# Attention with top-k masking and two feed-forward stages on one core: score fill, lead weights and the closing products of the first block are put in another order

## The chip, the cores and the metric

The program runs on one core of one Trainium2 chip. The metric is the device time of one execution in microseconds (us). Three runs of the kernel before gave 1180.0 us in the median, 1177.77 to 1182.78. A core has a matrix engine (PE, with its weight loads as PEld), a vector engine (DVE), a scalar engine (ACT), a general engine (POOL) and a queue engine (SP) from which the transfers are issued. Each engine takes its own instructions in order, and engines wait for each other by semaphores.

## The reference

Four batches with eight heads of 576 tokens and 64 dimensions go through attention that keeps, in each row of scores, the 32 largest; the result (2304 tokens by 512 features) goes through two feed-forward stages with 2048 hidden units each.

```python
scores = scale * np.matmul(q, k.transpose(0, 1, 3, 2))
kth = np.partition(scores, -top_k, axis=-1)[..., -top_k:-top_k + 1]
scores = np.where(scores >= kth, scores, -1000000000.0)
scores = scores - np.max(scores, axis=-1, keepdims=True)
attn = np.exp(scores)
attn = attn / (np.sum(attn, axis=-1, keepdims=True) + 1e-09)
x = np.matmul(attn, v)                 # then transposed to (2304, 512)
h = np.maximum(x @ w_in, 0.0)          # first stage
x = h * h @ w_out
h = x @ w_in                           # second stage, own weights
out = np.maximum(0.01 * h, h) @ w_out
```

## The kernel before, in words

**Tiles.** The tokens are cut into nine units (`UNITS`), each unit into four head pairs (`uh`), each head pair into tiles of 128 score rows by 576 keys. Two tiles make a pair, numbered `p`; there are 72 pairs. Products run in a split form: a high part and a rest, so that a value is carried in two matrices (`xh` and `xl`, two halves of `wi` and `wo`).

**One tile's way.** PE makes the scores into PSUM (`scores`, L310), ACT copies them to a score buffer `s0` to `s5` (L311). DVE searches the 32 largest in seven operations: MAX finds eight, MATCH_REPLACE strikes them out into `w`, four MAX and three MATCH_REPLACE in all (L951, L953). ACT drops what is below the 32nd (`drop`, L329) and takes the exponential (L333); PE transposes the result (`pt_main`, L369), ACT copies it to `PT` (L379), and PE multiplies it with the values (`av`, L455). `x_out` scales by the reciprocal sum (L486), and writes the features `xh` (ACT, L487) and `xl` (L493).

**Fill.** The scores of batches 2 and 3 (`EARLY`), and of the unit `KEPT`, are made ahead. PE makes them into the PSUM tag `sp`, ACT copies them to one of five buffers of the tag `stage`, and SP stores them to memory (`sd`, L314). They are spread evenly over the slots of `FILL`.

**Blocks.** The tokens make six blocks. The first has 512 tokens, and is complete after pair 15 (`first_done`). Its last pair is not masked and multiplied with the pair as a whole, but tile by tile in `close`: subtraction for the shift (L347, twice), drop, exponential, reciprocal (L351), transposes (L369, L355, L357). The value product of the last head pair is done in two halves: the first head with `hs` = (0,), the second with (1,). The copy that writes the last `xh` is noted as `closed`.

**Weights.** A stage of a block takes 16 steps, and each step needs a chunk `wi` and a chunk `wo`. Chunks arrive as 64-bit numbers (`w_raw`, 1 MB each, two buffers) and are made into the split form when first used: ACT reads the low words (L565) and the high words (L574), DVE joins them (`bits`, L581), ACT and POOL split (L585, L586). For steps 0 and 1 this is done ahead by `lead_passes` (L606, on ACT) and `lead_bits` (L613, on DVE). After that, `w_convert` of step i+2 runs beside the products of step i, and the raw chunk of step i+4 is asked for when step i is done. The low words of step 2 are held behind `closed`.

**What sets the order.** A table of slots (`at(slot, fn)`, 16 slots a pair) says when each function is called. Calls are handed to a scheduler, with priorities (`SOON`, `URGENT`, `SEAM`), which places the instructions of each engine one after the other. `behind(key)` (L86 ff.) ties an instruction to stand after a noted one. A change in the table therefore moves instructions on all engines, also far from the place that was edited.

## Time and profile before

| what | value |
|---|---|
| median of three runs | 1180.0 us |
| lowest and highest | 1177.77 and 1182.78 us |
| the profiled execution's own time | 1180.58 us |
| its span, first to last instruction | 1178.8 us |
| PE busy | 1118.3 us, 95% |
| DVE busy | 838.6 us, 71% |
| ACT busy | 818.0 us, 69% |
| POOL busy | 747.9 us, 63% |
| mean granted PE clock | 0.989 |

The rows further below are from one profiled execution, and starts are counted from its first instruction. Busy times are averages over stages: up to about 165 us there is attention and fill alone, then block 0 closes, then the feed-forward steps of one block run beside the attention of the next, and after about 900 us there are feed-forward steps alone. A row of the timeline merges equal neighbours (x2), and where an engine stood idle before it, the brackets say how long and what released it. A product with `PT` stands once in the order and has two rows in the trace (five are x10).

### The profile page before, as it was taken

How to read it: one execution, taken by the hardware profiler on the slowest of the kernel's cores; microseconds unless marked ns; L12 is line 12 of the kernel's file. 1: busy time of each engine (PE TensorE's matmuls, PEld its weight loads, DVE VectorE, ACT ScalarE, POOL GpSimd, SP SyncE). 2: the span in 40 equal slices, each digit the busy share in tenths (PEclk: the TensorE clock that was granted, in tenths of full speed). 3: DMA queues.
4: the chain of work that ended last, by engine and by line, in shares of the span. 5: the costliest groups of instructions: out<-in, count | busy, mean ns of one | idle time of the engine just before them, and what ended most of it. 6: DMA issues, size and time to landing. Idle time of an engine off the chain costs nothing.

```text
span 1178.8 us, 20036 instructions
## 1 busy us (share of the span) xinstructions
PE 1118.3 (95%) x6376; PEld 985.8 (84%) x6376; DVE 838.6 (71%) x1770; ACT 818.0 (69%) x1827; POOL 747.9 (63%) x958
## 2 busy tenths in 40 slices
PE   5898977998899999999999999999999999999998
PEld 4777765877688899989998998888788899998997
DVE  7999999666775659999999999989999100110011
ACT  6999998998999668877677677656866633333322
POOL 7968746998888767767897776768656543002100
PEclk9999989999999999999999999999999999999999
DMA  9868767999999688899988888667676499779974
GB/s 306 283 216 284 259 206 268 355 325 330 333 340 366 222 309 291 278 317 384 308 288 294 297 286 292 228 215 234 223 234 207 147 327 337 264 244 347 349 257 134
DMA packets 108201, 329.53 MB, mean 280 GB/s; under 512 B 17216, under 2 KB 25408, under 8 KB 104000
## 3 DMA queue, kind: packets, MB, share of 16 engines
q1 hardware_dynamic: 105472, 323.53, 80.0%
q10 hardware_dynamic: 2624, 4.72, 1.1%
q8 instruction: 52, 0.85, 0.3%
q14 instruction: 53, 0.43, 0.1%
HBM read 257.03 MB, written 71.17 MB: 278 GB/s over the span
## 4 chain that ended last, share of the span: by engine, by line
PE 78%; ACT 9%; DVE 4%; POOL 3%; DMA 2%; issue 2%; ACTq 0%; POOLq 0%; DVEq 0%
PE h L675 31%; PE acc L714 16%; PE acc L712 15%; PE att L466 5%; PE att L369 4%; PE att L455 2%; DVE m L951 2%; PE sp L310 2%; DVE w L953 2%; PE att L310 2%; DMA wraw<-in_w_dram 1%; ACT e L333 1%; ACT stage L311 1%; PE att L384 1%; ACT s L311 1%
## 5 line engine op out<-in xcount | busy, mean ns | idle before, releaser
L675 PE MATMUL h<-xh,wi 128*128 128x512 f32 (+2 forms) x1280 | 345.1, 343 | 6.3 <-ACT ga L685 2.3
L951 DVE MAX8 m<-w 128x8 f32<-128x576 f32 x432 | 311.4, 748 | 2.3
L675 PEld LDWEIGHTS h<-xh,wi 128*128 128x128 f32 x1280 | 225.3, 189 | 31.8 <-ACT ga L692 3.6
L695 POOL TENSOR_TENSOR gl<-ga,gh 128x512 fp32r<-128x512 f32 (+2 forms) x160 | 162.5, 1018 | 124.8 <-ACT gh L694 106.4
L953 DVE MATCH_REPLACE8 w<-m,w 128x576 f32<-128x576 f32 x288 | 213.1, 743 | 0.7
L675 PE MATMUL h<-xl,wi 128*128 128x512 f32 (+2 forms) x640 | 204.5, 340 | 0.0
L377 POOL TENSOR_TENSOR PTs<-whole,PTs 128x512 fp32r<-128x512 f32 x112 | 144.8, 1300 | 45.7 <-ACT whole L376 43.7
L712 PE MATMUL acc<-gh,wo 128*128 128x512 f32 (+2 forms) x768 | 155.6, 340 | 0.0
L714 PE MATMUL acc<-wo,gh 128*128 128x512 f32 x576 | 152.4, 397 | 0.0
L712 PEld LDWEIGHTS acc<-gh,wo 128*128 128x128 f32 x768 | 126.1, 189 | 11.3
L675 PEld LDWEIGHTS h<-xl,wi 128*128 128x128 f32 x640 | 120.2, 189 | 10.8
L329 ACT ACTIVATE e<-s,m 128x576 f32<-128x576 f32 x144 | 112.4, 782 | 21.0 <-DVE m L951 14.4
L695 DVE TENSOR_TENSOR gl<-ga,gh 128x384 fp32r<-128x384 f32 x32 | 17.9, 559 | 151.8 <-ACT gh L694 149.1
L692 ACT ACTIVATE ga<-h 128x512 f32<-128x512 f32 (+2 forms) x96 | 46.6, 492 | 112.0 <-PE h L675 109.7
L951 DVE MAX8 m<-s 128x8 f32<-128x576 f32 x144 | 104.4, 748 | 26.4 <-ACT s L311 24.3
L714 PEld LDWEIGHTS acc<-wo,gh 128*128 128x128 f32 x576 | 104.9, 188 | 20.1
L333 ACT ACTIVATE e<-e,nb 128x576 f32<-128x576 f32 x144 | 111.3, 778 | 3.0 <-POOL nb L323 2.8
L953 DVE MATCH_REPLACE8 w<-m,s 128x576 f32<-128x576 f32 x144 | 106.9, 744 | 0.4
L687 POOL TENSOR_TENSOR ga<-ga 128x512 f32<-128x512 f32 (+2 forms) x80 | 66.3, 831 | 42.7 <-ACT gh L686 40.8
L466 PE MATMUL att<-PTs,VT 128*128 128x256 f32 (+2 forms) x504 | 87.9, 299 | 4.1 <-DVE PTs L394 2.4
L369 PE MATMUL att<-ident,e 128*128 128x128 f32 x576 | 86.8, 275 | 4.8 <-ACT e L333 4.4
L364 POOL TENSOR_SCALAR e<-e,rc 128x576 f32<-128x576 f32 x112 | 82.9, 752 | 11.7 <-DVE rc L341 9.8
(109 smaller groups left out, 2069.7 us busy)
## 6 DMA issues: line engine op xcount, KB each, us to landing
wi<-wd SPq DMA_DIRECT2D x160, 512.0 KB, 5.3
wo<-wd SPq DMA_DIRECT2D x160, 512.0 KB, 5.2
wraw<-in_w_dram SPq DMA_DIRECT2D x32, 1024.0 KB, 7.8
sd<-stage SPq DMA_DIRECT2D x76, 288.0 KB, 3.2
s<-sd SPq DMA_DIRECT2D x76, 288.0 KB, 5.1
wd<-wi SPq DMA_DIRECT2D x32, 512.0 KB, 7.3
wd<-wo SPq DMA_DIRECT2D x32, 512.0 KB, 7.3
vd<-VT SPq DMA_DIRECT2D x16, 640.0 KB, 6.5
```

The source lines that it names most:

```text
L329: ACT.activation(t["e"], t["s"], AF.Prelu, bias=pr["m8"][:, i, 31:32], scale=-1.0, alpha=1.0 / FAR)
L333: ACT.activation(e, e, AF.Exp, bias=pr["nb"][:, i:i + 1], scale=-FAR, accum_out=pr["sum"][:, i:i + 1])
L364: POOL.tensor_scalar(e, e, pr["rc"][:, i:i + 1], 1.0, op0=OP.mult, op1=OP.mult)
L369: PE.transpose(ps[:, j * P:(j + 1) * P], t["e"][:, j * P:(j + 1) * P], ident)
L377: POOL.tensor_tensor(pts[:, 4:8, c:c + P], whole, pts.bitcast(F)[:, 0:4, c:c + P], op=OP.subtract)
L466: PE.matmul(ps, lhsT=l, rhs=r, start=i == 0, stop=i == len(mm) - 1)
L675: PE.matmul(two[r][:, 0:n], lhsT=ws[r][:, w, c * P:(c + 1) * P], rhs=x[c][y][:, 0:n], start=cnt == mine[0], stop=cnt == mine[-1])
L695: (DVE if j >= GLD else POOL).tensor_tensor(gl[:, 0:n], a[:, 0:n], gh.bitcast(F)[:, 0:n], op=OP.subtract)
L712: PE.matmul(acc[c][:, 0:n], lhsT=wo[:, w, cs], rhs=g[:, 0:n], start=first, stop=last)
L714: PE.matmul(acc[c], lhsT=g[:, cs], rhs=wo[:, w, :], start=first, stop=last)
L951: cur["dve"] = DVE.max(out=m8[:, x, 8 * r:8 * r + 8], in_=t["s"] if r == 0 else t["w"])
L953: cur["dve"] = DVE.match_replace(out=t["w"], in_to_replace=m8[:, x, 8 * r:8 * r + 8], in_values=t["s"] if r == 0 else t["w"], imm_value=NEG)
```

## The change

The fill of early scores ends at slot 205, where it ended at 222. The lead passes of steps 0 and 1 begin at slots 206 and 212 (before 224 and 230), with their loads 40 slots ahead of that as before. Their high words go to a buffer of the tag `stage` in SBUF, where they went to PSUM. The scores of pair 16 use the PSUM tag `sp`, those up to pair 15 the tag `sd`. The second head's half of the last value product of block 0 is cut into its two tiles (`av_tile`, `x_tile`): one tile is multiplied, scaled and written while the other is still on its way. Of pair 16, the first MAX of each tile stands behind the last shift as before; the further search stands behind the last `xl`, and its drops behind `closed`.

```diff
--- before.py
+++ after.py
@@ -47,7 +47,7 @@
 KEPT = 3
 
 EARLY = (2, 3)
-FILL = (2, 222)
+FILL = (2, 205)
 KPB = 2
 NST = 5
 SDB = 2
@@ -302,7 +302,9 @@
         mm = [(x[:, h, c:c + P], kt[:, h, ks]) for h, c in t["parts"] for x in d]
         if not direct(uh):
             ps = stage_psum.tile([P, 512], F, tag="sp", name="sp", bufs=SPB)
-        elif t["i"] // 2 <= first_done + 1 or kept(uh):
+        elif t["i"] // 2 == first_done + 1:
+            ps = stage_psum.tile([P, 512], F, tag="sp", name="sp", bufs=SPB)
+        elif t["i"] // 2 <= first_done or kept(uh):
             ps = stage_psum.tile([P, 512], F, tag="sd", name="sd", bufs=SDB)
         else:
             ps = bank()
@@ -326,7 +328,8 @@
     def drop(pr, i):
         t = pr["t"][i]
         t["e"] = ebufs[t["i"] % NE]
-        ACT.activation(t["e"], t["s"], AF.Prelu, bias=pr["m8"][:, i, 31:32], scale=-1.0, alpha=1.0 / FAR)
+        with behind("closed") if pr["p"] == first_done + 1 else ExitStack():
+            ACT.activation(t["e"], t["s"], AF.Prelu, bias=pr["m8"][:, i, 31:32], scale=-1.0, alpha=1.0 / FAR)
 
     def expo_sum(pr, i):
         e = pr["t"][i]["e"]
@@ -455,6 +458,14 @@
             PE.matmul(ps, lhsT=vt[0:np_, j, h * D:h * D + P], rhs=PT[0:np_, j, uh["c0"] + h * n:uh["c0"] + h * n + n],
                       start=m == 0, stop=m == len(order) - 1)
 
+    def av_tile(uh, t):
+        vt = VT[uh["b"], uh["hp"]]
+        uh["avt"] = bank()
+        for j in range(5):
+            np_ = P if j < NJ else LEFT
+            PE.matmul(uh["avt"][:, 0:P], lhsT=vt[0:np_, j, D:D + P], rhs=PT[0:np_, j, t["col"]:t["col"] + P],
+                      start=j == 0, stop=j == 4)
+
     def av_split(uh, h):
         n = uh["n"]
         c = slice(uh["c0"] + h * n, uh["c0"] + h * n + n)
@@ -470,6 +481,21 @@
         mine, other = slice(h * 64, h * 64 + 64), slice(64 - h * 64, 128 - h * 64)
         ACT.activation(uh["tmp"][mine, 0:n], ps[other], AF.Copy)
         DVE.tensor_tensor(uh["xf"][mine, 0:n], ps[mine], uh["tmp"][mine, 0:n], op=OP.add)
+
+    def x_tile(uh, t):
+        blk = blocks[cur["fill"]]
+        xh, xl = block_x(blk)[uh["hp"]]
+        r0 = (t["i"] - uh["ti"]) * P - uh["n"]
+        r, x = slice(D, P), early.tile([P, 256], F, tag="xn", name="xn", bufs=1)
+        d = slice(uh["u"]["g0"] - blk["g0"] + r0, uh["u"]["g0"] - blk["g0"] + r0 + P)
+        DVE.tensor_tensor(x[r, 0:P], uh["avt"][r, 0:P], uh["rb"][r, r0:r0 + P], op=OP.mult)
+        closed = ACT.activation(xh[r, d], x[r, 0:P], AF.Copy)
+        cur["xl"] = DVE.tensor_tensor(xl[r, d], x[r, 0:P], xh.bitcast(F)[r, d], op=OP.subtract)
+        if r0:
+            assert uh["u"]["g0"] + uh["n"] == blk["g0"] + blk["n"]
+            cur["closed"] = closed
+            ready.append(blk)
+            cur["fill"] += 1
 
     def x_out(uh, hs):
         g0, n, hp = uh["u"]["g0"], uh["n"], uh["hp"]
@@ -600,8 +626,7 @@
         for x, w in enumerate(w_alloc(i)):
             xs = slice(x * 512, x * 512 + 512)
             lo, hi, b = raw[:, xs, 0], raw[:, xs, 1], c[:, xs]
-            v = stage_psum.tile([P, 512], F, tag="sd" if len(led) == 2 and not led[i] else "sp", name="v",
-                                bufs=SDB if len(led) == 2 and not led[i] else SPB)
+            v = ahead.tile([P, S], F, tag="stage", name="v", bufs=NST)[:, 0:512]
             ACT.activation(b, lo, AF.Copy, scale=L_SCALE, bias=L_BIAS)
             ACT.activation(v, hi.bitcast(F), AF.Prelu, scale=H_SCALE, alpha=2.0 ** 32)
             led[i].append((b, v.bitcast(U), w))
@@ -881,9 +906,14 @@
         tight = uh["last"] // 2 == first_done
         apart = uh["n"] > P and (uh["n"] % P or tight) and uh["ti"] % 2 == 0
         for hs in ((0,), (1,)) if apart else ((0, 1),):
-            near = tight and hs[-1] == 1
+            near = tight and hs == (1,)
             z = 16 * (uh["lastA"] // 2 if hs == (0,) else uh["last"] // 2) + (15 if near else 23 if tight and apart else 30)
             nq = 2 * len(hs)
+            if near:
+                for i, t in enumerate(pairs[first_done]["t"]):
+                    at(z - 7 + 8 * i, urgent(av_tile), uh, t)
+                    at(z - 6 + 8 * i, urgent(x_tile), uh, t)
+                continue
             for i in range(nq):
                 at(z + i, urgent(av) if tight else av, uh, hs, i)
             at(z + nq, urgent(x_out) if tight else x_out, uh, hs)
@@ -900,7 +930,7 @@
         for _ in w_convert(i):
             pass
 
-    for i, z in enumerate((224, 230)):
+    for i, z in enumerate((206, 212)):
         at(z - 40, w_raw, i)
         at(z, lead_passes, i)
         at(16 * first_done + 13, lead_bits, i)
@@ -947,7 +977,7 @@
                 x, r, top = i // 7, i % 7 // 2, i % 7 % 2 == 0
             t = pr["t"][x % 2]
             if i < 14 and top:
-                with behind("shift") if p == first_done + 1 and r == 0 else ExitStack():
+                with behind("xl" if r else "shift") if p == first_done + 1 else ExitStack():
                     cur["dve"] = DVE.max(out=m8[:, x, 8 * r:8 * r + 8], in_=t["s"] if r == 0 else t["w"])
             elif i < 14:
                 cur["dve"] = DVE.match_replace(out=t["w"], in_to_replace=m8[:, x, 8 * r:8 * r + 8],
```

The first place is DVE, in the search of pair 13 (score buffers s2 and s3), during the attention ahead of the close. Before, from the first strike-out of s3 on:

```order
L951 MAX m8_2013<-w_2017 128x8
L951 MAX m8_2156<-w_2159 128x8
L953 MATCH_REPLACE w_2160<-m8_2156,s3_104 128x576
L953 MATCH_REPLACE w_2159<-m8_2156,w_2159 128x576
L951 MAX m8_2156<-w_2160 128x8
L951 MAX m8_2156<-w_2159 128x8
L953 MATCH_REPLACE w_2160<-m8_2156,w_2160 128x576
L953 MATCH_REPLACE w_2159<-m8_2156,w_2159 128x576
L341 RECIPROCAL rc_2015<-sum_2014 128x2
L486 TENSOR_TENSOR xn_2187<-att_2146,rb_1964 128x256
L951 MAX m8_2156<-w_2160 128x8
```

The same pair now:

```order
L983 MATCH_REPLACE w_2222<-m8_2219,w_2222 128x576
L981 MAX m8_2076<-w_2080 128x8
L981 MAX m8_2219<-w_2222 128x8
L983 MATCH_REPLACE w_2223<-m8_2219,s3_104 128x576
L983 MATCH_REPLACE w_2222<-m8_2219,w_2222 128x576
L981 MAX m8_2219<-w_2223 128x8
L981 MAX m8_2219<-w_2222 128x8
L983 MATCH_REPLACE w_2223<-m8_2219,w_2223 128x576
L981 MAX m8_2219<-w_2223 128x8
L983 MATCH_REPLACE w_2223<-m8_2219,w_2223 128x576
L981 MAX m8_2219<-w_2223 128x8
```

Before, operations on the two tiles of the pair, or on those of a neighbouring pair, take turns. Now tile `w_2223` has five operations in a row, each of which reads what the one ahead of it has written.

The second place is PE, from the transposes of block 0's last pair (e2 and e3 are its two tiles, `VN` the values, `rc` the reciprocal sums) to shortly ahead of the first feature product. Before:

```order
L369 MATMUL att_2448<-ident_66,e2_109 128x128
L455 MATMUL att_2460<-PT_115,VN_1110 128x256 x5
L369 MATMUL att_2448<-ident_66,e2_109 128x128 x3
L355 MATMUL sp_2454<-ident_66,e2_109 64x128
L369 MATMUL att_2481<-ident_66,e3_110 128x128 x4
L355 MATMUL sp_2487<-ident_66,e3_110 64x128
L357 MATMUL sp_2454<-ident_66,rc_2400 128x128
L455 MATMUL att_2504<-PT_115,VN_1110 128x256 x4
L310 MATMUL att_2531<-KT_1731,q00_77 128x288
L310 MATMUL att_2531<-KT_1731,q10_78 128x288
L455 MATMUL att_2504<-PT_115,VN_1110 128x256
L357 MATMUL sp_2487<-ident_66,rc_2400 128x128
```

Now (L458 is the product of the first head, L466 that of one tile, L372, L358 and L360 are the transposes):

```order
L372 MATMUL att_2448<-ident_66,e2_109 128x128 x4
L358 MATMUL sp_2454<-ident_66,e2_109 64x128
L408 MATMUL att_2434<-ident_66,rc_2324 128x128 x2
L458 MATMUL att_2460<-PT_115,VN_1144 128x256 x5
L466 MATMUL att_2467<-PT_115,VN_1144 128x128 x5
L360 MATMUL sp_2454<-ident_66,rc_2400 128x128
L358 MATMUL sp_2497<-ident_66,e3_110 64x128
L372 MATMUL att_2491<-ident_66,e3_110 128x128 x4
L360 MATMUL sp_2497<-ident_66,rc_2400 128x128
L466 MATMUL att_2520<-PT_115,VN_1144 128x128 x5
L312 MATMUL att_2541<-KT_1784,q00_77 128x288
L312 MATMUL att_2541<-KT_1784,q10_78 128x288
```

The first head's product stood within the transposes of tile e2, and a product of 256 columns closed the row; now the tile products stand one behind the copy of e2, one behind that of e3.

The third place is ACT, where `ga` of step 2 (L685, now L710) stands among the high words (L574, now L600). The chunk `wraw_2672` was that of step 5, `wraw_2625` that of step 4. Before:

```order
L574 ACTIVATE att_2709<-wraw_2625 128x512
L585 ACTIVATE wi_2680<-wc_2682 128x512
L329 ACTIVATE e3_110<-s5_106,m8_2777 128x576
L574 ACTIVATE att_2746<-wraw_2672 128x512
L574 ACTIVATE att_2770<-wraw_2672 128x512
L685 ACTIVATE ga_2703<-h_2676 128x512
L129 ACTIVATE VT_3114<-vraw_3115 128x5x64 x2
L686 ACTIVATE gh_2701<-ga_2703 128x512
```

Now `wraw_2635` is the chunk of step 4 and `wraw_2682` that of step 5:

```order
L710 ACTIVATE ga_2713<-h_2686 128x512
L600 ACTIVATE att_2702<-wraw_2635 128x512
L600 ACTIVATE att_2719<-wraw_2635 128x512
L591 ACTIVATE wc_2692<-wraw_2635 128x1024
L711 ACTIVATE gh_2711<-ga_2713 128x512
L336 ACTIVATE e0_107,sum_2515<-e0_107,nb_2760 128x576
L336 ACTIVATE e1_108,sum_2515<-e1_108,nb_2760 128x576
L600 ACTIVATE att_2756<-wraw_2682 128x512
```

The two reads of the chunk of step 5 stood ahead of `ga` and `gh` of step 2; now the first of them is seven rows behind that `ga`, and the second follows it.

## Rows read from the trace of the kernel before

**Rows 1.** The page: the span.

```profile
span 1178.8 us, 20036 instructions
```

**Rows 2.** Busy time by stretch: stretch, length, PE, PEld, DVE, ACT, POOL, PE clock, DMA share, GB/s.

```profile
10.00:165.00 155.00, 135.45 (x786) 111.42 (x785) 154.07 (x334) 141.92 (x393) 120.12 (x179) 0.99 0.78 258
165.00:210.00 45.00, 34.02 (x137) 25.81 (x135) 40.91 (x86) 38.05 (x86) 29.97 (x34) 0.85 0.78 271
210.00:330.00 120.00, 110.15 (x516) 89.87 (x515) 83.48 (x156) 108.97 (x207) 108.60 (x110) 0.97 0.94 336
330.00:900.00 570.00, 564.53 (x3316) 504.51 (x3315) 517.24 (x1111) 421.05 (x913) 422.58 (x531) 1.00 0.82 282
```

**Rows 3.** Waits of DVE, 9 to 170 us: total us, times, longest us.

```profile
DVE m L951 <- ACT s L311: 1.8, 3, 1.3
```

**Rows 4.** Timeline of DVE around the last search: start, duration, engine, line, operation, operands, count.

```profile
157.76 0.74 DVE L951 MAX8 m<-s 128x8 f32<-128x576 f32 x1
158.42 0.07 DVE L953 MATCH_VALUE_LOAD w<-m,s 128x8 f32 x1
...
159.21 0.74 DVE L953 MATCH_REPLACE8 w<-m,w 128x576 f32<-128x576 f32 x1
159.87 1.41 DVE L951 MAX8 m<-w 128x8 f32<-128x576 f32 x2
...
168.98 0.16 DVE L347 TENSOR_TENSOR nb<-m 128x1 f32<-128x1 f32 x1
...
172.57 0.76 DVE L951 MAX8 m<-w 128x8 f32<-128x576 f32 x1
173.37 0.09 DVE L953 MATCH_VALUE_LOAD w<-m,w 128x8 f32 x1
173.44 0.74 DVE L953 MATCH_REPLACE8 w<-m,w 128x576 f32<-128x576 f32 x1
174.22 0.76 DVE L951 MAX8 m<-w 128x8 f32<-128x576 f32 x1
```

**Rows 5.** ACT by line and shape, 60 to 160 us: count, total busy us, mean ns, idle before.

```profile
L311 ACT ACTIVATE stage<-sp 128x288 f32<-128x288 f32 x100 | 35.5, 434 | 2.2 <-PE sp L310 1.9
```

**Rows 6.** Timeline of ACT at the close of block 0.

```profile
172.97 0.81 ACT L333 ACTIVATE e<-e,nb 128x576 f32<-128x576 f32 x1
...
177.39 0.60 ACT L379 ACTIVATE PT<-att 128x512 f32<-128x512 f32 x1 [2.74 <-PE att L369]
...
182.88 0.41 ACT L487 ACTIVATE xh<-xn 64x256 fp32r<-64x256 f32 x1
```

**Rows 7.** Timeline of PE at the close; in brackets its idle time and what ended it.

```profile
156.65 2.52 PE L455 MATMUL att<-PT,VN 128*128 128x256 f32 x10
...
164.64 1.04 PE L369 MATMUL att<-ident,e 128*128 128x128 f32 x8
...
173.14 3.74 PE L455 MATMUL att<-PT,VN 128*128 128x256 f32 x10
...
182.27 2.08 PE L675 MATMUL h<-xh,wi 128*128 128x512 f32 x8
```

**Rows 8.** Busy time by stretch: five us in which the PE clock fell.

```profile
170.00:175.00 5.00, 3.78 (x10) 2.73 (x11) 4.48 (x10) 4.66 (x13) 4.35 (x5) 0.50 0.93 326
```

**Rows 9.** Timeline of PE, its three long waits after the first feature products.

```profile
191.18 0.53 PE L310 MATMUL att<-KT,q 128*128 128x288 f32 x2 [2.39 <-DVE wc L581]
...
200.45 1.20 PE L712 MATMUL acc<-gl,wo 128*128 128x512 f32 x4 [2.26 <-POOL gl L695]
...
205.70 0.50 PE L675 MATMUL h<-xh,wi 128*128 128x512 f32 x1 [1.92 <-ACT ga L685]
```

**Rows 10.** Timeline of ACT, the wait for the raw weights.

```profile
203.95 1.18 ACT L574 ACTIVATE att<-wraw 128x512 f32<-128x512 f32 x2 [2.61 <-DMA wraw<-in_w_dram]
```

**Rows 11.** Timeline of the SP queue, raw weights of steps 4 and 5.

```profile
189.36 0.45 SPq L543 DMA_DIRECT2D wraw<-in_w_dram  x1
...
195.16 0.35 SPq L543 DMA_DIRECT2D wraw<-in_w_dram  x1
```

## The prediction

> **What bounds the kernel now.** I read the busy times by stretch first, then the timelines of DVE, PE and ACT where one engine hands over to another, and at each place the wait that ends last. The span [rows 1] is 1178.8 of the 1180.58 us of the profiled execution, with 1.8 us around it, which I leave as they are. The sum below is made against 1180.58, which is 0.6 us above the median of 1180.0.
>
> Three regimes follow each other [rows 2]. From 10 to 165 us DVE is busy 154.07 of 155 us: the search sets the time. PE has 19.6 us to spare there, but ACT only 13.1. From 165 to 210 us no engine is full. Block 0 closes, PE is idle 11.0 of 45 us and runs at a mean granted clock of 0.85. From 210 us on PE is the engine to look at: 110.15 of 120 us, then 564.53 of 570. What PE gets earlier at 210 us should therefore reach the end, unless a later stage gives it back. DVE is busy 517.24 of those 570 us too, but it has 36.5 us free between 210 and 330 us, so work pushed there finds room.
>
> So the change can earn in the 45 us of the close, and can lose in the search ahead of it.
>
> **Part 1: the search ahead of the close.** Fill copies move forward. In ACT's order, the score copies of pairs 10 to 15 now have 6 to 10 more fill copies ahead of them than before, at 0.36 us each (35.5 us for 100) [rows 5]: 2.2 to 3.6 us of ACT work. The work is the same in sum. Before, DVE waited for a score copy three times, 1.8 us in all and 1.3 at most [rows 3], so ACT was just in time, and this is a cost where ACT falls behind DVE.
>
> But DVE falls behind as well. What shows it is how its operations follow each other [rows 4]. Where the next operation works on another tile, MAX is followed after 0.66 us (157.76 to 158.42), MATCH_REPLACE after 0.66 (159.21 to 159.87). Where the next one reads what this one wrote, it is 0.80 (172.57 to 173.37) and 0.78 (173.44 to 174.22). Such a link costs 0.12 to 0.14 us. Before the second shift, DVE's order had 2 of them; now it has 21, as the first of the order pieces shows. The operations are the same in number, and there is no idle time to take it up: 19 x 0.13 = 2.5 us, later by that. Bounds: 0, if the next tile would have been waited for anyway, and 5 us, if the copies make DVE wait as well (two more waits of 1.3 [rows 3]). I take +2.5, since the two delays run side by side.
>
> The Trainium skill, "VectorE: DVE Perf Modes", section "The DRAIN you can't avoid", says that after every vector operation the pipe is flushed before the next begins, and that chaining does not change this. By that a link costs nothing, and this part is 0. The trace does not agree: 0.66 against 0.80 and 0.78.
>
> **Part 2: the close.** Before, the second shift is done at 168.98 [rows 4], and the last xh starts at 182.88 [rows 6]: 13.9 us. What lay in it: the second exponential starts only at 172.97, since ACT had four high words of the lead passes (now earlier) in its queue; the value product of the first head took 3.74 us [rows 7] at a granted clock of 0.50, its lower level of 1.2 GHz [rows 8], where 2.52 us was its time at the full clock; and the product of the second head, with all 256 columns, waited for both tiles.
>
> Now, counted from the second shift: the first head's product needs the last copy of pair 14, which stands in ACT's order behind the first exponential; of its 0.60 [rows 6] some 0.4 is still to run. First head, ten passes, 3.1 us (between 2.52 and 3.74): 3.5. Product of the first tile, half the columns: 1.6, to 5.1. ACT has meanwhile run the second drop and exponential (0.8 each), ready by 3. Transposes of the second tile and of its reciprocal, seven at 0.13 (1.04 for eight): 6.0. Copy 0.6: 6.6. Product of the second tile 1.6: 8.2. Scaling on DVE, one score copy queued ahead of it on ACT, then xh, some 0.4 each [rows 6]: 9.4. With hand-overs that I can't price from a row, 10.5. That saves 3.4. Bounds: 0, if PE stays at the half clock throughout and ACT's copies come late, and 5.4, if PE runs at the full clock (8.5).
>
> The feature products need the last xh only after sixteen of them; they started at 182.27 [rows 7], so they are held by PE's own queue, and go as the tile products go.
>
> **Part 3: steps 2 to 5 of the first stage.** After that, PE waits three times for long [rows 9]: 2.39 us for a bank that DVE's joining of the words of step 2 frees, 2.26 for POOL's rest of the hidden values, 1.92 for ACT's ga. Together 6.57. The third is a transfer. ACT stood 2.61 us at the high words of step 5 [rows 10], whose load was issued at 195.16 [rows 11], with ga of step 2 queued behind it. In ACT's order now, ga and gh of step 2 stand ahead of that read, so this wait leaves PE's path. The first is covered as well: on PE the products of wo of step 0 now stand ahead of those of step 2. The second stays: POOL still has wi and wo of step 2 to split beside the hidden values. 2.39 + 1.92 = 4.3 us off. Bounds: 0, if POOL or the transfer takes the place, and 6.6.
>
> The wait that is added: pair 16's search stands behind the last xl, and eight of its operations stand ahead of the joining of step 2 on DVE, 5.4 us at 0.66 to 0.73. ACT's wi, POOL's split and PE's products of step 2 wait for them. PE has the eight products with wo of step 0 meanwhile, about 2 us, so I count nothing; without that cover it is up to 3 us, which is in the upper bound of part 3 (nothing saved). Pair 16's own drops come later, and nobody waits for them before DVE's free time [rows 2].
>
> **Edits at nothing.** The high words hold four of the five stage buffers until DVE has read them, so the last fill copy waits for a store: hidden by the wait for the second shift, else one wait like the longest of rows 3, 1.3 us. The other PSUM tag for pair 16 takes no instruction away.
>
> **Sum.** +2.5 - 3.4 - 4.3 = -5.2. 1180.58 - 5.2 = 1175.4 us, 4.6 us (0.39%) below the median.
>
> **The rivals.** About 0.5%, 5.9 us, is what a measurement of this kernel can tell from no change: below 1174.1 is faster, above 1185.9 slower.
>
> All three waits go, and PE gets its clock back. The stretch 165 to 210 lacks 15% of 45 us of clock [rows 2], 6.8 us; a third of it is 2.2. +2.5 - 3.4 - 6.6 - 2.2 = -9.7: 1170.9. For it: worked through queue by queue, step 3 comes earlier by more than my sum. Against it: POOL's queue is no shorter.
>
> The gain is given back by 330 us. In that stretch ACT is busy 108.97 and POOL 108.60 of 120 us, and the transfers 0.94 [rows 2]. If these set the pace of the steps rather than PE, and the new order of the whole program lines them up worse by 5 us (half as much again as PE's 9.85 us of idle time there), it is 1180. For it: the order changes on every engine well past the close. Against: an earlier start of the same steps moves transfers forward too, into 165 to 210, where they were at 0.78.
>
> Slower: the search waits for score copies. Place: the first MAX of each tile of pairs 10 to 15, 12 of them. Price: 0.9 us each, two to three fill copies [rows 5], 10.8 in all, as ACT has little free time [rows 2]. 10.8 + 2.5 - 7.7 = +5.6: 1186.2. It decides from about 0.4 us a tile on, where the gains are used up. Against it: the copies of the last pair have the same total work ahead of them as before, so ACT can't lose 11 us on the whole unless it also stands idle more.
>
> Links cost nothing, as when each operation is followed after the same time whatever it reads: part 1 is 0, 1172.9. The rows speak against it. This is the skill's rule of part 1.
>
> **How the numbers follow.** The forecast has 0.38 (its own range 1172 to 1179; 0.08 of it lies below 1174.1). All waits gone 0.27, given back 0.21, slower 0.09, links free 0.05. Faster: 0.27 + 0.08 + 0.05 = 0.40. Slower 0.09, and 0.01 from the given-back case: 0.10. The same: 0.50. Range: lower end 1167, below the second case by some of its bounds (all of parts 2 and 3 at their best, 5.4 and 6.6, without part 1, is 1168.6, and the clock beside it), upper end 1183, which leaves the search's case out: about 2 in 10 outside.
>
> **What would show it.** The second shift at about 171.5 us where it was at 168.98, DVE still without idle time and its MAX rows at 0.8 where they follow their own strike-out; the last xh about 10.5 us behind the shift; no ACT wait for wraw ahead of ga of step 2, and the first feature product of step 3, at 205.70 before [rows 9], at about 200.5. From there the gap between both timelines should stay near 5 us up to the end. It is wrong if the second shift is on time (links free) or past 175 (copies late), if PE's waits in rows 9 are replaced by others of their size, or if the gap at 200 us and the gap at the end differ by more than 3 us.

## The result, and the profile after

The changed kernel takes 1195.3 us (median of 6 runs, 1191.94 to 1197.53) against 1180.63 for the one before (6 runs beside them): ratio 1.0114, interval 1.0087 to 1.0141. It is slower by 14.7 us where 5.2 us of gain were forecast. Its profiled execution took 1192.64 us.

The busy time by stretch, with the columns of [rows 2]:

```profile
10.00:165.00 155.00, 133.13 (x760) 108.49 (x760) 147.23 (x315) 137.90 (x383) 114.19 (x171) 0.98 0.77 257
165.00:210.00 45.00, 36.12 (x170) 28.76 (x168) 40.07 (x84) 36.18 (x85) 31.50 (x34) 0.89 0.66 233
210.00:330.00 120.00, 111.10 (x509) 89.51 (x508) 88.02 (x168) 111.46 (x212) 111.30 (x114) 0.96 0.96 340
330.00:900.00 570.00, 558.22 (x3264) 497.87 (x3264) 517.02 (x1106) 417.86 (x909) 418.63 (x527) 0.99 0.82 280
```

Two places stand out. In the search DVE, full before, is idle for 7.8 of 155 us and has done 19 instructions fewer. And from 330 us on PE has lost 6.3 us of busy time and some clock. The close between them got better, as far as PE goes: 36.12 us busy at a mean granted clock of 0.89, where it was 34.02 at 0.85.

**The search.** These are DVE's waits from 9 to 180 us (total, times, longest), 9.0 us in all:

```profile
DVE m L981 <- ACT s L313: 4.5, 3, 2.2
DVE rc L344 <- POOL sum L343: 3.3, 3, 2.6
DVE rc L344 <- ACT sum L341: 0.7, 1, 0.7
DVE m L981 <- POOL nb L325: 0.5, 1, 0.5
```

Before, they were 2.0 us: the 1.8 of [rows 3] and one more line of the same view:

```profile
DVE rc L341 <- POOL sum L340: 0.2, 1, 0.2
```

The timeline of DVE, as in [rows 4], at the second shift and the close:

```profile
177.75 0.76 DVE L981 MAX8 m<-w 128x8 f32<-128x576 f32 x1
178.54 0.16 DVE L350 TENSOR_TENSOR nb<-m 128x1 f32<-128x1 f32 x1
...
182.00 2.48 DVE L638 SCALAR_TENSOR_TENSOR wc<-v,wc 128x512 uint32<-128x512 uint32 x2
...
188.74 0.29 DVE L491 TENSOR_TENSOR xn<-att,rb 64x128 f32<-64x128 f32 x1 [3.20 <-POOL xl L519]
...
190.47 0.29 DVE L493 TENSOR_TENSOR xl<-xn,xh 64x128 fp32r<-64x128 f32 x1 [0.37 <-ACT xh L492]
```

The second shift comes at 178.54 and not at 168.98: 9.56 us late, of which 2.5 were forecast.

**The close and the first steps.** The timeline of PE, as in [rows 7, 9]:

```profile
179.64 3.25 PE L458 MATMUL att<-PT,VN 128*128 128x256 f32 x10
182.82 1.57 PE L466 MATMUL att<-PT,VN 128*128 128x128 f32 x10
...
185.88 1.57 PE L466 MATMUL att<-PT,VN 128*128 128x128 f32 x10 [0.25 <-ACT PT L382]
...
187.75 2.00 PE L700 MATMUL h<-xh,wi 128*128 128x512 f32 x8
...
197.33 0.53 PE L312 MATMUL att<-KT,q 128*128 128x288 f32 x2 [2.87 <-ACT s L313]
...
207.47 0.39 PE L700 MATMUL h<-xh,wi 128*128 128x512 f32 x1
```

The first feature product is 5.5 us later than before (187.75, was 182.27), the first of step 3 only 1.8 us (207.47, was 205.70). So by 207 us the feed-forward products had made good most of the 9.56 us. The search of the next block had not: the strike-out that DVE began at 210.55 us before is 9.4 us late.

**Far behind it.** Here the rows show something that the prediction did not look at. First two stretches of the kernel before, then the same two of the changed one:

```profile
540.00:570.00 30.00, 30.00 (x192) 28.90 (x192) 29.66 (x66) 22.19 (x49) 25.01 (x36) 1.00 0.98 359
...
640.00:670.00 30.00, 30.00 (x171) 27.25 (x170) 29.79 (x65) 21.32 (x47) 21.85 (x28) 1.00 0.90 302
```

```profile
540.00:570.00 30.00, 25.78 (x161) 23.48 (x160) 28.80 (x64) 21.14 (x49) 21.00 (x30) 1.00 0.90 329
...
640.00:670.00 30.00, 26.38 (x138) 23.73 (x137) 27.68 (x61) 20.02 (x46) 20.30 (x27) 0.89 0.73 245
```

Before, PE was full at its upper clock in both. Now it is idle 4.2 and 3.6 us, and the clock of the second is 0.89; on 26.38 us of busy time that is another 2.9 us by my estimate. The clock fell after PE had stood idle for 2.15 us; from 645 to 650 us it is 0.53, near the lower of its two levels (1.2 GHz):

```profile
646.70 1.65 PE L700 MATMUL h<-xh,wi 128*128 128x384 f32 x4 [2.15 <-DVE xl L752]
```

```profile
645.00:650.00 5.00, 3.30 (x10) 3.30 (x11) 4.94 (x11) 1.81 (x5) 1.46 (x3) 0.53 0.75 258
```

What it waits for in the first, from PE's timeline, and the SP queue at that time:

```profile
549.03 0.96 PE L700 MATMUL h<-xh,wi 128*128 128x384 f32 x4 [1.40 <-DMA wi<-wd]
...
557.10 0.38 PE L477 MATMUL att<-PTs,VT 128*128 128x256 f32 x1 [1.20 <-ACT PTs L377]
558.43 0.97 PE L700 MATMUL h<-xh,wi 128*128 128x384 f32 x4 [0.95 <-ACT xh L513]
```

```profile
548.27 0.32 SPq L320 DMA_DIRECT2D s<-sd  x1
555.71 0.32 SPq L656 DMA_DIRECT2D wo<-wd  x1
```

At 549 a new block of tokens begins (its products are 384 columns wide). Part of its first products need features that the attention is only just finishing (xh of L513). SP issues nothing for 7.4 us; its next load, of `wo`, waits 7.3 of them for PE (L387, a transpose). In the order of before, the same products began at 547.83, behind the last of these features (xh at 545.51).

To follow this through the runs I took the same event in each trace: the second shift, then the first `gl` of the first stage (199.12 us before), and the `gl` that were at 326.53, 537.10, 732.35 and 1170.00. They follow the feed-forward steps; the column "search" follows the attention by DVE's strike-out that was at 536.27. The table has the difference to before in us, and the ratio of the times. A trace is one execution; executions of one kernel differ by up to 10.0 us, so offsets below 4 us say little at the end, and the ratios decide there.

| run | shift | 199 | 327 | search | 537 | 732 | 1170 | ratio (interval) |
|---|---|---|---|---|---|---|---|---|
| changed kernel | +9.6 | +2.0 | +3.4 | +7.8 | +1.1 | +13.2 | +12.0 | 1.0114 (1.0087 to 1.0141) |
| e1 fill205 | +10.0 | +3.8 | +7.1 | +14.2 | +12.8 | +19.8 | +18.8 | 1.0135 (1.0117 to 1.0152) |
| e2 close_only | +2.2 | -6.1 | -0.1 | +4.1 | +4.2 | +4.1 | +5.3 | 1.0040 (1.0025 to 1.0054) |
| e3 dup_early | +10.8 | +13.4 | +9.4 | +10.7 | +10.7 | +10.4 | +8.8 | 1.0069 (1.0055 to 1.0084) |
| e4 close_xn | +2.0 | -5.2 | -1.0 | -0.2 | -0.2 | -0.1 | -0.6 | 1.0009 (0.9992 to 1.0025) |
| e5 fewer_stores | +0.4 | +0.4 | -4.9 | -4.1 | -4.0 | -4.1 | -4.8 | 0.9989 (0.9973 to 1.0006) |
| e6 close_fewer | +0.2 | -7.7 | -3.5 | -2.1 | -2.1 | -2.1 | -1.7 | 1.0011 (0.9995 to 1.0026) |
| e7 reorder | +1.7 | +2.2 | +0.4 | +4.9 | -1.7 | +9.5 | +8.3 | 1.0088 (1.0064 to 1.0111) |
| e8 sum_on_act | +11.3 | +4.3 | +16.4 | +20.2 | +20.2 | +20.2 | +20.3 | 1.0171 (1.0150 to 1.0192) |
| e9 links | +10.7 | +4.9 | +8.2 | +14.5 | +3.5 | +15.0 | +14.7 | 1.0105 (1.0081 to 1.0130) |
| e10 late_order | +3.0 | +3.4 | -0.8 | +8.1 | -2.0 | +13.4 | +11.6 | 1.0067 (1.0047 to 1.0088) |
| e11 no_hold | +0.4 | -6.0 | -2.9 | -1.2 | -1.3 | -1.2 | -1.2 | 0.9993 (0.9978 to 1.0009) |
| e12 fill206 | +8.4 | +1.5 | +4.9 | +4.4 | +4.4 | +4.3 | +4.0 | 1.0031 (1.0013 to 1.0049) |
| e13 fill202 | +11.2 | +4.3 | +7.1 | +7.4 | +7.4 | +7.4 | +8.6 | 1.0066 (1.0047 to 1.0086) |

The changed kernel's columns around 537 are the first surprise: its feed-forward was nearly level there, and its search was 7.8 us late. Behind that point the feed-forward had to wait for it.

The traces also show from where on a run has the instruction order of before again. In e2 to e6, e8 and e11 to e13 that is so on every engine from 490 us on at the latest. In these nine both columns agree within 0.1 us, and the offset changes by -1.8 to +1.2 us from 537 to 1170. The changed kernel, e1, e7, e9 and e10 have another order up to about 950 us or longer. In these five the search is 1.4 to 11 us further behind than the feed-forward at 537, and the offset grows by 6.0 to 13.7 us up to 1170.

### The profile page after: what moved, and what is told of

Read it like the earlier page. It is cut to its first block, busy times and chain, and to the rows that moved or that the text cites. A ratio compares the mean times of both kernels' runs of the same rounds, so it can differ in the third digit from the quotient of the medians.

```text
span 1190.9 us, 20042 instructions
## 1 busy us (share of the span) xinstructions
PE 1125.3 (94%) x6386; PEld 989.4 (83%) x6386; DVE 841.9 (71%) x1772; ACT 817.5 (69%) x1828; POOL 747.3 (63%) x958
## 4 chain that ended last, share of the span: by engine, by line
PE 63%; ACT 11%; DVE 8%; DMA 7%; POOL 3%; issue 3%; ACTq 0%; POOLq 0%; SPq 0%; DVEq 0%
PE h L700 26%; PE acc L739 16%; PE acc L737 9%; DVE m L981 4%; PE att L477 4%; DVE w L983 3%; PE att L372 3%; DMA wraw<-in_w_dram 3%; ACT e L336 2%; PE att L458 2%; ACT stage L313 1%; ACT e L332 1%; DMA wi<-wd 1%; PE sp L312 1%; ACT s L313 1%
## 5 line engine op out<-in xcount | busy, mean ns | idle before, releaser
L700 PE MATMUL h<-xh,wi 128*128 128x512 f32 (+2 forms) x1280 | 346.2, 345 | 10.6 <-ACT ga L710 3.2
L700 PEld LDWEIGHTS h<-xl,wi 128*128 128x128 f32 x640 | 120.5, 190 | 10.5
L739 PEld LDWEIGHTS acc<-wo,gh 128*128 128x128 f32 x576 | 105.2, 188 | 20.3 <-ACT gh L719 0.3
L372 PE MATMUL att<-ident,e 128*128 128x128 f32 x576 | 89.8, 278 | 10.5 <-ACT e L336 9.7
```

The lines of the kernel that those rows point to most:

```text
L372: PE.transpose(ps[:, j * P:(j + 1) * P], t["e"][:, j * P:(j + 1) * P], ident)
L700: PE.matmul(two[r][:, 0:n], lhsT=ws[r][:, w, c * P:(c + 1) * P], rhs=x[c][y][:, 0:n], start=cnt == mine[0], stop=cnt == mine[-1])
L739: PE.matmul(acc[c], lhsT=g[:, cs], rhs=wo[:, w, :], start=first, stop=last)
```

## The experiments

**Which edit, and is it the search?** The theory was that the search's delay is carried to the end by DVE (A), the rivals that PE carries the close's gain (P), or that the new order behind the close does the harm (B).

```diff
-FILL = (2, 222)
+FILL = (2, 205)
```

> The kernel before with one number changed: the fill copies are spread up to slot 205 and not 222; the close, the lead passes and the holds are those of before. Theory A (the search carries it: what DVE is late by at the second shift reaches the end, because DVE is full again from about 450 us on): second shift near 178 us instead of 168.98, the close takes its 13.9 us as before, end 1190 us or a little more, ratio 1.008 to 1.010. Theory B (the loss of the change comes from the new order after the close, not from the search): second shift late all the same, but the end within 3 us of 1180.6. Theory C (the search is late because of the lead passes and the pair behind the close, not because of the fill): second shift before 172 us and the end at 1180.

This one number on the kernel before makes the search 10.0 us late and the whole 1.35% slower. So the fill alone is enough for the search's delay, without the lead passes or the holds (C falls). But the offset of 12.8 at 537 us grew to 19.8 at 732: more than A has.

```diff
-FILL = (2, 205)
+FILL = (2, 222)
```

> The changed kernel with the fill put back to slot 222: the close by tiles, the early lead passes and the holds stay. Theory A (search carries): second shift back at 169 to 170 us, the last xh 2 to 4 us earlier than before, and the end still at 1179 to 1181 us, since the blocks after the first wait for the attention and not for the close. Theory P (PE carries from 210 us on, as the prediction had it): the gain of the close and of the first steps reaches the end: 1173 to 1176 us. Theory B (the order after the close does it): between 1185 and 1195.

All the other edits without the fill: the features lead by 6.1 us at 199, as the prediction's parts 2 and 3 had it, and the lead is gone at 327. P falls: 1.0040, not a gain. Behind 537 us the offset stays within 1.2 us.

```diff
                     cur["dve"] = DVE.max(out=m8[:, x, 8 * r:8 * r + 8], in_=t["s"] if r == 0 else t["w"])
+                if 10 <= p < 14 and 0 < r < 3:
+                    with behind("dve"):
+                        DVE.max(out=spare, in_=t["w"])
```

> The kernel before with sixteen more MAX instructions in the search of pairs 10 to 13, whose results go to a spare tile that nobody reads: 16 x 0.66 = 10.6 us of DVE work ahead of the close, and the order of all engines after the close is that of before. Theory A and theory P: second shift at 177 to 180 us, and the whole of the delay at the end: 1189 to 1192 us, ratio 1.007 to 1.010. Theory B (a late close is made up again in DVE's 36 us of free time between 210 and 330 us): 1180 to 1183.

Time lost in the search does reach the end, for the most part: 10.8 us at the shift, 10.7 at 537, 8.8 at 1170, ratio 1.0069. DVE's idle time between 210 and 330 us makes up little of it. By this A holds, and alone it would explain some three fifths of the loss. One reservation: the order was expected to be that of before, and on every engine it differs from it up to about 485 us.

```diff
-        r, x = slice(D, P), early.tile([P, 256], F, tag="xn", name="xn", bufs=1)
+        r, x = slice(D, P), uh["xn"][:, r0:r0 + P]
...
             x = early.tile([P, 256], F, tag="xn", name="xn", bufs=1)
+            uh["xn"] = x
```

> As the close-only kernel, and the two products of the second head write their scaled values into the buffer that the first head's half already has, so the second scaling does not wait for POOL to have read it (3.20 us of DVE in the changed kernel). Last xh 2 to 3 us earlier than in the close-only kernel. Theory A: the end does not follow it, 1179 to 1181 us, within 0.1% of the close-only kernel. Theory P: 2 to 3 us less than the close-only kernel, 1170 to 1174.

This run missed its aim. In e2, POOL was done with the buffer in time and DVE did not wait for it, so there was nothing to take away (both runs have the fill of before): the first feature product comes 10.6 us after the shift, where it came 10.8. The 4 us between the ends of e2 and e4 arose at 340 us, with another order of DVE and ACT in between, and say nothing of the buffer.

**Where the lead of the close goes.** Theory T: the transfers, at 0.94 of their time from 210 to 330 us [rows 2], set the pace. e5 leaves out six stores on the kernel before, e6 on e4; the later blocks then load another step's weights, so part of the result is other (as in e7).

```diff
+    LEFT_OUT = [(0, f) for f in (9, 10, 11, 12, 13, 14)]
+    for layer, f in LEFT_OUT:
+        wdram[layer, f] = wdram[layer, 2]
...
+        if steps[i][1:] in LEFT_OUT:
+            return
```

> The kernel before, leaving out the stores of the split weights of steps 9 to 14 of the first layer (6 MB written between about 250 and 310 us; the later blocks load step 2's weights in their place, the same bytes, so part of the result is other). The order on the compute engines is that of before, instruction for instruction. Theory T (from 210 to 330 us the transfers set the pace of the steps): the first block's first layer ends 5 to 9 us earlier at 308 us, and this stays to the end: 1172 to 1176 us. Rival E (PE, ACT and POOL set the pace there): within 1 us of before at 308 us and at the end.

> The same six stores left out of the close-only kernel with the shared buffer; its order on the compute engines stays too. That kernel was 5.4 us ahead of before at 199 us, 1.2 us at 327 us and 0.8 us at the end. Theory T (the lead is lost to transfers that were full anyway): the lead over the kernel before with the same stores left out stays 3 us or more at 327 us and at the end. Rival E (the lead is lost on PE's order, where feature products stand between search and transposes that are late): no lead over it at the end, within 1 us.

T falls. The transfers' share from 210 to 330 us went from 0.94 to 0.82, and the time did not move (0.9989, e6 1.0011). The single trace of e5, the fastest of its twelve runs, shows 4 us; the twelve do not. e6 led by 7.7 us at 199 and by 2.1 at 537, no more than e5.

**The order of the late part.** Leaving out another set of stores moved the order of all engines far behind the close, and that was the run that turned the case.

```diff
+    LEFT_OUT = [(0, f) for f in (7, 9, 11, 13)]
+    for layer, f in LEFT_OUT:
+        wdram[layer, f] = wdram[layer, f - 1]
```

> The kernel before, leaving out the stores of steps 7, 9, 11 and 13 of the first layer (4 MB). With this set the late part of the order (from about 700 us on, and much of 450 to 700) comes out as in the kernel of before with the fill up to slot 205, while the search ahead of the close is that of before. Theory A alone (only what DVE is late by at 450 us counts): at 504 us not later than before, and the same offset at the end, 1172 to 1181 us. Theory B as a second part (the new order costs some 5 us of its own between 550 and 850 us): the offset grows by 4 to 7 us between 537 and 833 us, end 1180 to 1186 us.

Less work, a search within 1.7 us at the shift, feed-forward 1.7 us ahead at 537 (its search 4.9 behind), and then 11 us lost up to 732: 1.0088. B holds as a second cause, and in this trace its price is about twice what I had written down.

```diff
+    TWICE = [(0, f) for f in (8,)]
+    again = dram.tile([P, 4, 512], F, tag="again", name="again")
...
+        if steps[i][1:] in TWICE:
+            SP.dma_start(again[:, 0:2, :], wi.bitcast(F))
+            SP.dma_start(again[:, 2:4, :], wo.bitcast(F))
```

> The kernel before with the split weights of step 8 of the first layer stored twice, the second time to a place that nobody reads (1 MB more). With this the order of all engines from about 700 us on, and of PE from 550, is the one of the changed kernel; everything up to the close is that of before. Theory B as second part (the late order costs by itself): level with before at the second shift, within 4 us at 450 us, and an offset that grows by 4 to 8 us between 560 and 840 us; end 1185 to 1192. Theory A alone (only the offset of DVE at 450 us counts): no growth behind 450 us, end 1179 to 1184.

This has none of the changed kernel's edits, and its order from about 730 us on. It departs from the order of before at about 250 us, and between there and 690 us the two are only in part alike. It is 2 us ahead at 537 with the feed-forward, though 8.1 behind with the search, and 13.4 behind at 732. The ratio is 1.0067, 8.0 us; the trace is of the slowest of its six executions. In its rows the same two stretches give way, here of e10:

```profile
540.00:570.00 30.00, 24.79 (x128) 22.59 (x128) 25.41 (x56) 18.37 (x41) 17.86 (x25) 0.83 0.76 283
...
640.00:670.00 30.00, 27.43 (x153) 24.89 (x152) 29.69 (x65) 21.11 (x48) 22.77 (x33) 0.94 0.76 255
```

The place belongs to the order, not to the kernel: e7, whose order is a third one, keeps PE busy for 29.19 and 30.00 us of these two stretches, and loses elsewhere (65.99 of 70 us from 670 to 740).

**Both together.** The last pair asks the reverse: the changed kernel with its late search, but with the late order of before (from 490 us on; in e13, with 202, from 400 us on).

```diff
-FILL = (2, 205)
+FILL = (2, 206)
```

> The changed kernel with the fill up to slot 206 and not 205: one slot of 222, and every other edit stays. Up to pair 14 the orders are nearly those of the changed kernel (its second shift should come at 175 to 179 us), but from about 420 us on the order of all engines is that of before. Theory A alone (the search's delay carries, the late order is not what counts): like the changed kernel, 1192 to 1197 us. Theory B alone (the late order is the whole loss): 1179 to 1184. Both, each worth some 0.6 to 0.8% alone (late order of before with a search made 10 us late: 1.0069; late order of the changed kernel with a search on time: 1.0067): 1185 to 1190 us, and an offset that stays constant from 500 us on.

> The changed kernel with the fill up to slot 202: the copies are still earlier, and from about 240 us on the order of PE is that of before, of DVE from 420 on. By both theories together: the second shift at 174 to 179 us, the offset at 504 us what the search is late by, less up to 4 us that the close and the first steps give back, and constant from there: 1184 to 1190 us. Theory B alone: 1179 to 1183.

One slot of the fill takes 1.0114 to 1.0031: 1184.7 us, just under the 1185 to 1190 that I expected of "both". Its search is 8.4 us late, and the offset is 4.3 us from 537 to 890 and does not grow. The two stretches of e12:

```profile
540.00:570.00 30.00, 29.83 (x190) 28.02 (x189) 29.74 (x65) 22.31 (x52) 24.51 (x32) 1.00 1.02 388
...
640.00:670.00 30.00, 28.83 (x165) 26.07 (x166) 29.73 (x66) 20.11 (x46) 23.15 (x31) 1.00 0.88 295
```

e13, with a search 11.2 us late, ends at 1.0066 and is flat from 537 to 890 as well.

**What makes the search late.** Two runs. In e8 the 1e-9 is added on ACT for pairs 8 to 13:

```diff
-        if pr["p"] == first_done - 1:
+        if 8 <= pr["p"] <= first_done - 1:
             ACT.activation(pr["sum"], pr["sum"], AF.Copy, bias=1e-9)
```

> The changed kernel, where the sums of pairs 8 to 13 get their 1e-9 on ACT and not on POOL, so DVE's reciprocal no longer stands behind POOL's queue (3.3 us of waits in the changed kernel). If the second shift is late by waits for POOL: it comes at 175 to 176 us, 3 us earlier than the 178.54 of the changed kernel. If the 19 dependent links and the score copies make it late: 177 to 179 us. The end follows, 1187 to 1195 us, since the order after the close changes as well.

```profile
DVE m L981 <- ACT s L313: 7.1, 4, 4.0
DVE m L981 <- POOL q L131: 2.1, 1, 2.1
DVE rc L344 <- ACT sum L341: 1.2, 2, 0.7
DVE m L981 <- POOL nb L325: 0.3, 1, 0.3
DVE xn L512 <- ACT rb L423: 0.2, 1, 0.2
DVE rc L344 <- POOL sum L343: 0.2, 1, 0.2
```

The wait for POOL's sum went from 3.3 to 0.2 us, and the waits for score copies from 4.5 to 7.1: the shift came at 180.32, not earlier. Taking POOL out of this place did not bring the search forward. The edit gives ACT, whose copies DVE waits for, more to do, so it does not clear POOL altogether. The rest of e8 is worth as much: it is the slowest run of all (1.0171), with the order of before from 490 us on. It loses 16 us between 199 and 537, 12 of them up to 327. So what is placed between the close and 490 us can cost as much again; no run here separates it.

In e9 the searches of pairs 9 to 12 go tile by tile:

```diff
-            if p == first_done:
+            if p == first_done or 9 <= p < 13:
                 x, r, top = i // 7, i % 7 // 2, i % 7 % 2 == 0
...
-                with behind("shift") if p == first_done + 1 and r == 0 else ExitStack():
+                with behind("shift") if p == first_done + 1 and r == 0 else behind("dve") if 9 <= p < 13 else ExitStack():
                     cur["dve"] = DVE.max(out=m8[:, x, 8 * r:8 * r + 8], in_=t["s"] if r == 0 else t["w"])
             elif i < 14:
-                cur["dve"] = DVE.match_replace(out=t["w"], in_to_replace=m8[:, x, 8 * r:8 * r + 8],
+                with behind("dve") if 9 <= p < 13 else ExitStack():
+                    cur["dve"] = DVE.match_replace(out=t["w"], in_to_replace=m8[:, x, 8 * r:8 * r + 8],
```

> The kernel before, where the searches of pairs 9 to 12 go tile by tile, each operation held behind the one before it: DVE's order has 41 dependent links ahead of the second shift where it had 2; the score copies stand on ACT nearly as before. If a link costs what the rows show (0.13 us): 39 x 0.13 = 5.1 us, the second shift at 173 to 175 us. If links are free: 169 to 170. The order after the close changes too, so the end says little: 1180 to 1195 us.

```profile
DVE rc L341 <- POOL sum L340: 3.4, 3, 1.3
DVE m L951 <- POOL nb L323: 1.5, 2, 1.2
DVE m L951 <- ACT s L311: 1.2, 1, 1.2
DVE xn L486 <- ACT rb L420: 0.7, 1, 0.7
DVE m L951 <- ACT e L329: 0.5, 1, 0.5
DVE xn L486 <- PE att L455: 0.2, 1, 0.2
```

The shift is 10.7 us late, twice what 39 links give. But the waits sum to 7.5 us and were 2.4 from 9 to 181 us before; without these 5.1 us there remain 5.6 for 39 links, 0.14 each, the size read in [rows 4]. So the price of a link came out right, as a remainder, and the miss is the same as in the changed kernel: a search in another order also meets waits.

**Without the hold.** The edit is made on e4.

```diff
-                with behind("xl" if r else "shift") if p == first_done + 1 else ExitStack():
+                with behind("shift") if p == first_done + 1 and r == 0 else ExitStack():
...
-        with behind("closed") if pr["p"] == first_done + 1 else ExitStack():
+        if True:
```

> The close-only kernel with the shared buffer, without the holds on pair 16 (its search waits for the second shift alone, as before, and its drops for nothing); from about 450 us on its order is that of before. That kernel was 5.4 us ahead with the features at 199 us, but 5.7 us behind with the attention at 212 us. If the lead of the features is bought with the attention's delay by the hold: here the attention is at most 3 us behind at 212 us, the features at most 3 us ahead at 199 us, and the end is the same as with the hold, 1180 to 1184 us. If the hold is a cost that nothing pays for: attention level at 212 us, features still 4 us ahead, end 1175 to 1179 us.

Neither expectation came out. DVE's search is level at 212 us (0.2 us ahead) and the features still lead by 6.0 at 199, so the hold did not buy the lead; but the end is 0.9993, the same as before. It is the fastest form found with the close by tiles, 1.2% under the changed kernel (1180.48 against 1195.3 us), and no faster than the kernel before. None of the thirteen runs beats that one by more than its interval.

## Why the prediction was wrong, point by point

- **Part 1, the search (+2.5 forecast, +9.56 measured).** The links were sized right (0.14 in e9). Their number is less sure: the piece of DVE's order ahead of the prediction has four operations of `w_2223` in a row, not five, and by time the traces have 7 successions of 0.74 us or more (start to start, without a wait) before and 22 in the changed kernel, 15 more where 19 were counted. The step that failed is "I take +2.5, since the two delays run side by side": DVE's waits rose from 2.0 to 9.0 us and added to the links, 7.0 + 19 x 0.14 = 9.7. My upper bound of 5 allowed two more waits of the kind already seen; waits for POOL's sum, up to 2.6, were not in it. By the rule that the prediction weighed (the Trainium skill, "VectorE: DVE Perf Modes", "The DRAIN you can't avoid") e9 would have no cost of links; the trace does not agree, 5.6 us for 39. The same section says, what the prediction left out, that a next operation which is not held starts earlier; the 0.66 us between starts in [rows 4], where one operation takes 0.74, agree with that. With POOL taken out of the sums the search was no earlier (e8). That the copies put forward push everything else on ACT and PE back is what remains, argued and not shown.
- **Part 2, the close (-3.4 forecast, -2.3 measured).** The last xh starts 11.6 us behind the shift, where it was 13.9 and 10.5 were forecast:

```profile
190.13 0.31 ACT L492 ACTIVATE xh<-xn 64x128 fp32r<-64x128 f32 x1 [0.75 <-DVE xn L491]
```

  PE's products had the forecast size: 3.25 and twice 1.57 us where 3.1 and 1.6 were taken. Yet e1, with the close of before, needs 8.9 us from the shift to the first feature product and the changed kernel 9.2. Before it was 13.3, and with tiles, early lead passes and the fill of before it is 9.7 to 10.8 (e2, e4, e6, e11). So either edit, the earlier fill or the tiles with the early lead passes, shortens the close by 2.5 to 4.4 us, and both together (9.2, and 11.1 and 10.5 in e12 and e13) give no more than one; I had counted one gain and not asked which edit brings it. The buffer's wait of 3.20 was missed; the first feature product, at 187.75, had started before it ended at 188.74, and beyond that it was not tested.
- **Part 3, the first steps (-4.3 forecast).** The mechanism held: in e2, e4, e6 and e11 the features lead by 5.2 to 7.7 us at 199, and the changed kernel makes up 3.5 us between 187 and 199. In it the wait for raw weights ahead of ga of step 2 [rows 10] is gone, as forecast; ACT now reads them without a wait:

```profile
205.11 0.60 ACT L710 ACTIVATE ga<-h 128x512 f32<-128x512 f32 x1
205.59 1.20 ACT L600 ACTIVATE att<-wraw 128x512 f32<-128x512 f32 x2
```

  In place of 2.39 us for a bank, PE now waits 2.87 for a score copy, which I had not seen coming: the sign of being wrong "PE's waits in rows 9 are replaced by others of their size" is there for this one.
- **"What PE gets earlier at 210 us should therefore reach the end": this is the step that fails first.** Leads of 5.2 to 7.7 us at 199 end as 1.0040, 1.0009, 1.0011 and 0.9993. That was the rival "given back by 330 us", at 0.21. Its cause was to be the transfers or ACT and POOL. The transfers are refuted (e5, e6), and so is the hold as a cause (e11); what takes the lead between 199 and 400 us stays open. A delay, on the other hand, is mostly not given back (e3).
- **The order behind the close: not in the sum at all.** I wrote in a rival that "the order changes on every engine well past the close", and priced it at 5 us up to 330 us. In the changed kernel the feed-forward lost 1.4 us from 199 to 327, and the most at 540 to 570 and 640 to 670 us. Another order far behind the close costs 1.0067 by itself (e10), and 0.8% lie between e12 and the changed kernel. What in the order does it is read from PE's waits in two stretches, and not isolated.
- **The slower rival** (score copies, 10.8 us, at 0.09) named the search's place and nearly its size; its waits were for POOL and ACT both. Its end of 1186.2 lies beside e12 and e13, which have the late order of before.
- **The sum as it was.** With the late order of before, the late search costs 0.31% (e12, 8.4 us late) to 0.66% (e13, 11.2 us late); the 9.56 us of the changed kernel lie between. The new order costs 0.67% alone (e10). Together that is 0.98 to 1.33%, and 1.14% was measured. The prediction had named "past 175" for the shift and a change of more than 3 us between 200 us and the end as its failures, and both are there: 178.54, and +2.0 against +12.0. The forecast range of 1167 to 1183 held no case with a loss of both kinds.

## What to carry to other kernels

Where a scheduler sets the order of a whole program, an edit early on can draw the order of everything behind it anew, and a tuned kernel may stand on a good draw; all five runs with a new late order lost time behind 537 us. So compare the orders stretch by stretch, and before pricing an edit ask whether the late part is still the old one. A one-step change of a constant (205 to 206 here) or a neutral edit that brings in only the new order separates the two prices. A lead made in one stretch is worth something only if the stretch behind it can take it, while a delay in an engine that is full later is mostly passed on (8.8 of 10.8 us in e3), so gains and losses at the same place must not be set off against each other one to one.

## What the runs showed of the hardware

Before, the high words that DVE joins lay in PSUM; the changed kernel has them in SBUF, so both inputs of that operation (L638 now, L613 before) are in SBUF. The row at 182.00 above shows two of them in 2.48 us. What POOL did beside it:

```profile
181.00 2.94 POOL L640 TENSOR_TENSOR wi<-wc,wi 128x512 fp32r<-128x512 f32 x2
```

Before, one of them ran beside the same splitting on POOL, here DVE and then POOL:

```profile
171.12 0.69 DVE L613 SCALAR_TENSOR_TENSOR wc<-v,wc 128x512 uint32<-128x512 uint32 x1 [0.42 <-ACT v L606]
```

```profile
170.54 1.27 POOL L615 TENSOR_TENSOR wi<-wc,wi 128x512 fp32r<-128x512 f32 x1
```

So 1.24 us each where it was 0.69 beside POOL. Both inputs in SBUF alone do not make it slow; with POOL idle until 179.40, one took 0.69 in the changed kernel too:

```profile
178.62 0.69 DVE L638 SCALAR_TENSOR_TENSOR wc<-v,wc 128x512 uint32<-128x512 uint32 x1
```

The Trainium skill, "SBUF — State Buffer", section "Who interferes with whom", says that a DVE instruction with two SBUF inputs contends with a GpSimd instruction that reads SBUF, since its second input comes through the shared read interface. The trace agrees with it: 1.24 against 0.69. Whether these 1.1 us reached the end was not tested.
